# Scores of the output factor through SBUF, and the exponentials of a batch in one place of each engine's order

## The chip, the core and the metric

The kernel runs on one core of a Trainium2 chip as one program. The metric is the device time of an execution in microseconds (us). Five engines work from queues of their own: TensorE (PE), VectorE (DVE), ScalarE (ACT), GpSimd (POOL) and SyncE (SP), which here issues the transfers. The kernel writes the order of the instructions on each engine itself; at run time an instruction starts when its engine is free and the semaphores that it waits for have come.

## The reference

```python
# q, k, v: (4, 8, 576, 64)
q_lm, k_lm = means of 18 neighbouring rows            # 32 landmarks
A  = sm(q, k_lm); Bm = sm(q_lm, k_lm); C = sm(q_lm, k) # sm: max subtracted, exp, divided by sum
Z  = Bm.T / (norm1(Bm) * norminf(Bm) + 1e-6)
for _ in range(6): Z = 2 * Z - Z @ Bm @ Z
x  = A @ Z @ C @ v                                     # then rows of (2304, 512)
h  = x @ w_in;  x = (h * cos(h)) @ w_out               # d_ff 2048
h  = x @ w_in2; return (max(h, 0) + alpha * min(h, 0)) @ w_out2
```

## The kernel before

**Stages.** Four batches go through attention and through the first pair of layers. Each batch has two units of four heads (`unit(u, ...)`, units 0 and 1 for batch 0, 2 and 3 for batch 1, and so on) and one landmark matrix with its iterations (`z_path(b, ...)`). A unit transposes k and q (L594), forms the scores of the factor C (L670, "scores of the output factor": landmark queries against all keys), takes their maximum and exponential (L685 to L694), transposes the exponentials (L700, L704) and multiplies them by v (L715). It then forms the scores of A and their softmax (L742 to L757). `z_path` makes B, and iterates on it and on the product of C and v together: L851 is one Newton-Schulz step, and the first of these steps needs both units' products of L715. The weight that leaves `z_path` gives the operands of L909, and these feed the layers.

**Ticks.** The first pair of layers is cut into 128 ticks, each with six L949 matmuls into a PSUM tile `h`, an ACT and DVE chain for h cos(h) (L954 k, L956, L958 Sin, L959 square, L960, L963), and twelve L976 matmuls into `acc`. The tile `h` has two buffers: L949 of a tick waits for L960 of two ticks earlier. The units and the `z_path` of batches 1 to 3 are worked on between ticks: batch 1 from the start, batches 2 and 3 from ticks 36 and 66. The second pair of layers (L1235, L1316) follows.

**The planner.** Nothing of this order is written by hand. `Plan.op` takes operations with the buffers they read and write, `after` adds orders that no buffer forces, and `Plan.go` (L114) repeatedly picks, of the operations that are ready, the one that its table of durations lets start first, with a small term for its due time. An operation that needs another ACT function set than the current one is lengthened by 1.28 and its due time moved (L217). So a change of durations, of buffers or of `after` moves instructions on every engine.

**ACT function sets.** Exp belongs to one set and Sin to another. When consecutive ACT operations need different sets, an ACT_TABLE_LOAD stands between them.

**The tile `raw`.** It has three places, taken in turn by all its users: the loads of weights that are to be converted (`convert`, L465: 512 KB each, then three DVE operations L471, L473, L475), and, for batches 1 to 3, the k, q and v of each unit (L552, L568, L569). A place is taken again when the last reader of its user is done: L475 for a weight, L594 for k and q, L715 for v. All these loads go through the one queue that SP issues from, in order.

Of the kernel before, what the change touches and what calls it, by code (L numbers as in the profile page):

```python
# [258 lines left out]
def kernel(  # L259
# [267 lines left out]
    def unit(u, tu):  # L527
# [159 lines left out]
        op(dve(2), lambda e: nc.vector.tensor_reduce(nm_.t, mx.t, axis=AX.X, op=ALU.max, negate=True),  # L687
           r=[mx], w=[nm_])
        ce = atb(m, "ce", [P, R0, 2, 64])
        for ch in range(2):  # L690
            n = (N0, N1)[ch]
            op(("ACT", n / 1200.0 + 0.18), lambda e, ch=ch, n=n: nc.scalar.activation(
                ce.t[:, 0:n // 64, ch, :], sc[ch].t[:, 0:n].rearrange("p (r s) -> p r s", s=64),
                AF.Exp, bias=nm_.t, accum_out=sm.t[:, ch:ch + 1]), r=[sc[ch], nm_], w=[ce, sm], aset="exp")  # L694
# [66 lines left out]
    def z_path(b, tz):  # L761
# [620 lines left out]
```

## Time and profile before

| | |
|---|---|
| time, median of 3 runs | 882.39 us (881.43 to 885.32) |
| the profiled execution | 881.18 us |
| its span, first to last instruction | 879.4 us |
| busy: PE / DVE / ACT / POOL | 825.8 / 646.4 / 483.9 / 198.2 us |
| mean granted TensorE clock | 0.984 |

The busy time of PE says how long some matmul was in flight, not how fast it went. Where PE is idle or its clock is below 1.00, another engine or a transfer was late. The stretches that matter here are from 72 us (where the changed order first differs) to some 376 us (where the attention of batch 3 is over).

### The profile page before, as it was taken

The numbers are of one execution on the slowest core, as the hardware profiler recorded it, in microseconds if no ns is written. First come the engines' busy times: TensorE is split into PE (matmuls) and PEld (weight loads), VectorE is DVE, ScalarE is ACT, GpSimd is POOL, SyncE is SP. The second block draws the span as 40 slices with busy tenths as digits, with TensorE's granted clock in tenths as the row PEclk, the third lists the DMA queues.
The fourth block names the chain that finished last, engine by engine and source line by source line (L and its number), as shares of the span: only waits on it lengthen the run. The fifth ranks groups of instructions, "written<-read, shape, count | busy, mean of one in ns | idle before, by whom it ended". The sixth has DMA issues, their size and how long they took to land.

```text
span 879.4 us, 15395 instructions
## 1 busy us (share of the span) xinstructions
PE 825.8 (94%) x5681; PEld 726.3 (83%) x5681; DVE 646.4 (74%) x1279; ACT 483.9 (55%) x1118; POOL 198.2 (23%) x220
## 2 busy tenths in 40 slices
PE   5677899999999998999989999999999999999997
PEld 4436789888798887897889888889999999999996
DVE  4989969987896889768998777775665566555563
ACT  4467757777875687667678534443344334333431
POOL 1224511333321332114432222200120012000110
PEclk8989999999999999999999999999999999999999
DMA  8476506775359846666555111140113011310231
GB/s 233 116 215 143 171 26 189 229 178 136 123 159 268 230 119 196 186 182 218 182 185 181 51 48 48 61 132 25 37 61 85 25 37 60 85 37 25 66 115 24
DMA packets 89051, 107.44 MB, mean 122 GB/s; under 512 B 35984, under 2 KB 63120, under 8 KB 88976
## 3 DMA queue, kind: packets, MB, share of 16 engines
q1 hardware_dynamic: 88976, 106.46, 41.2%
q8 instruction: 44, 0.72, 0.3%
q14 instruction: 31, 0.25, 0.1%
HBM read 82.06 MB, written 24.38 MB: 121 GB/s over the span
## 4 chain that ended last, share of the span: by engine, by line
PE 61%; DVE 19%; DMA 10%; issue 3%; ACT 3%; SPq 1%; POOL 1%; DVEq 0%; POOLq 0%; ACTq 0%
PE acc L1316 21%; PE acc L976 10%; PE h L1235 9%; PE x L1235 7%; PE h L949 5%; DMA m<-in_moe_w_in_dram 4%; DMA m<-in_moe_w_out_dram 3%; DVE m L323 3%; DVE m L475 3%; DVE m L473 3%; PE x L909 2%; DMA m<-wi2d 2%; DVE m L471 2%; DVE m L960 2%; DVE m L956 2%
## 5 line engine op out<-in xcount | busy, mean ns | idle before, releaser
L976 PE MATMUL acc<-m,m 128*128 128x288 f32 x1536 | 238.0, 301 | 7.0 <-DVE m L323 3.4
L323 POOL TENSOR_TENSOR m<-m,m 128x288 fp32r<-128x288 f32 (+3 forms) x129 | 126.0, 984 | 459.7 <-ACT m L963 233.5
L976 PEld LDWEIGHTS acc<-m,m 128*128 128x128 f32 x1536 | 213.7, 190 | 18.4 <-issue 7.7
L1316 PE MATMUL acc<-m,m 128*128 128x512 f32 x864 | 207.5, 392 | 0.7 <-DVE m L323 0.4
L323 DVE TENSOR_TENSOR m<-m,m 128x512 fp32r<-128x512 f32 (+4 forms) x271 | 170.3, 651 | 34.9 <-ACT m L1184 9.3
L1316 PEld LDWEIGHTS acc<-m,m 128*128 128x128 f32 x864 | 158.9, 189 | 31.9 <-DVE m L323 0.9
L949 PE MATMUL h<-m,m 128*128 128x288 f32 x768 | 131.8, 307 | 14.9 <-DVE m L960 12.8
L949 PEld LDWEIGHTS h<-m,m 128*128 128x128 f32 x768 | 109.6, 191 | 34.9 <-DVE m L960 19.9
L1304 ACT ACTIVATE m<-m 128x512 fp32r<-128x512 f32 (+1 forms) x80 | 46.3, 588 | 111.5 <-DVE m L1302 109.0
L1235 PE MATMUL h<-m,m 128*128 128x256 f32 x768 | 106.9, 282 | 0.7 <-ACT m L318 0.6
L1235 PEld LDWEIGHTS h<-m,m 128*128 128x128 f32 x768 | 99.7, 189 | 3.6 <-ACT m L318 1.3
L1258 DVE TENSOR_TENSOR m<-h,m 128x512 f32<-128x512 f32 x32 | 22.1, 690 | 81.8 <-ACT m L318 78.9
L1235 PE MATMUL x<-m,m 128*128 128x256 f32 x576 | 80.3, 283 | 1.7 <-ACT m L318 1.7
L963 ACT ACTIVATE m<-m 128x288 fp32r<-128x288 f32 x128 | 55.8, 441 | 40.5 <-DVE m L960 35.4
L1235 PEld LDWEIGHTS x<-m,m 128*128 128x128 f32 x576 | 73.1, 188 | 3.4 <-ACT m L318 1.9
L318 ACT ACTIVATE m<-h 128x256 f32<-128x256 f32 (+2 forms) x93 | 36.8, 396 | 67.2 <-PE h L1235 58.9
L958 ACT ACTIVATE m<-m 128x288 f32<-128x288 f32 x128 | 55.6, 440 | 26.4 <-DVE m L956 26.0
L960 DVE SCALAR_TENSOR_TENSOR m<-m,h 128x288 f32<-128x288 f32 x128 | 56.5, 446 | 15.1 <-ACT m L959 14.8
L1095 ACT ACTIVATE m<-m 128x512 fp32r<-128x512 f32 x68 | 41.4, 628 | 45.0 <-PE h L1235 19.4
L954 ACT ACTIVATE m<-h 128x288 int32<-128x288 f32 x128 | 51.4, 404 | 22.8 <-PE h L949 22.0
L956 DVE SCALAR_TENSOR_TENSOR m<-h,m 128x288 f32<-128x288 f32 x128 | 57.0, 448 | 3.4 <-ACT m L954 3.2
L959 ACT ACTIVATE m<-m 128x288 f32<-128x288 f32 x128 | 55.2, 439 | 2.4
(150 smaller groups left out, 897.5 us busy)
## 6 DMA issues: line engine op xcount, KB each, us to landing
m<-in_moe_w_in_dram SPq DMA_DIRECT2D x32, 512.0 KB, 5.4
m<-in_moe_w_out_dram SPq DMA_DIRECT2D x32, 512.0 KB, 4.4
m<-wi2d SPq DMA_DIRECT2D x56, 256.0 KB, 3.5
m<-w1d SPq DMA_DIRECT2D x32, 256.0 KB, 5.5
y1d<-m SPq DMA_DIRECT2D x24, 288.0 KB, 2.8
out_dram<-m SPq DMA_DIRECT2D x36, 128.0 KB, 2.4
w1d<-m SPq DMA_DIRECT2D x16, 256.0 KB, 5.3
wi2d<-m SPq DMA_DIRECT2D x16, 256.0 KB, 2.9
```

Of the source, the lines that this page charges most:

```text
L323: ENG[e].tensor_tensor(o, a, b, op=ALU.subtract)
L949: nc.tensor.matmul(out=hp.t[:, 0:CW], lhsT=w_[:, js], rhs=x[:, cs], start=(i == 0), stop=(i == 5))
L954: op(act(CW, True), lambda e: nc.scalar.activation(k_.t, hp.t[:, 0:CW], AF.Copy, scale=INV2PI), r=[hp], w=[k_], target=T + 0.8)
L956: op(dve(CW), lambda e: nc.vector.scalar_tensor_tensor(u.t, hp.t[:, 0:CW], INV2PI, k_.t, op0=ALU.mult, op1=ALU.subtract), r=[hp, k_], w=[u])
L958: op(act(CW), lambda e: nc.scalar.activation(u.t, u.t, AF.Sin, scale=math.pi), rw=[u], aset="sin")
L959: op(act(CW), lambda e: nc.scalar.activation(u.t, u.t, AF.Square, scale=math.sqrt(2.0)), rw=[u])
L960: op(dve(CW), lambda e: nc.vector.scalar_tensor_tensor(hc.t, u.t, 1.0, hp.t[:, 0:CW], op0=ALU.subtract, op1=ALU.mult, reverse0=True), r=[h ...
L963: op(act(CW), lambda e: nc.scalar.activation(gh.t, hc.t, AF.Copy), r=[hc], w=[gh, gl])
L976: nc.tensor.matmul(out=yg[o].t[:, 0:CW], lhsT=w_.t[:, sl], rhs=x.t, start=(j == ja and i == 0), stop=(j == jb and i == 2),)
L1235: nc.tensor.matmul(out=rv(k), lhsT=a_.t[:, p, c2, js], rhs=b_.t[:, q_, c2, 0:hw], start=(first and c2 == 0 and i == 0), stop=(c2 == 1 and ...
L1304: op(act(w), lambda e, m_=m_, gh=gh: nc.scalar.activation(gh.t[:, 0:w], m_.t[:, 0:w], AF.Copy), r=[m_], w=[gh, gl])
L1316: nc.tensor.matmul(out=ya[n][t].t, lhsT=gv(x_), rhs=r_.t, start=(st and k == 0), stop=(en and k == 2))
```

## The change

In the units of batches 1 to 3 (`m` is 1 there) the scores of C no longer stay in PSUM until their exponential is done. Each half is copied to the SBUF tile `ce` by ACT or DVE, one reduction over all 576 columns gives the negated maximum (before: two maxima in PSUM and one over the pair), and one exponential in place, with its sum accumulated, takes the place of two. Room for a second `ce` comes from `wt`, which goes from four to two buffers.

New `after` orders per batch: the first exponential of C waits for the maximum of the second unit and for the subtraction in `z_path`; the second exponential of C follows the first; the first exponential of A waits for the subtraction of the second unit; the second unit's transposes follow the first's; the loads of v come behind the loads of k and q of both units. An ACT operation that needs another function set while it is not yet due gets 1.0 added to its key in the planner (`SP`). Units 0 and 1 keep their computation.

```diff
+KN: SP=1.0
                     key = s + KA * min(dl - s, KC)
+                    if o.aset and o.aset != cur and o.dl > s:
+                        key += KN["SP"]
...
-    at = at_raw = lay(0, at, ("wt", 4, 1024))
+    at = at_raw = lay(0, at, ("wt", 2, 1024), ("cex", 1, CE))
...
-        loads(4, ldv, 1.64, w=[vn], after=aft)
+        marks["vl", b, c] = loads(4, ldv, 1.64, w=[vn], after=aft)
...
+            if m:
+                ce = ce or atb(m, "ce", [P, R0, 2, 64])
+                op(pe(n, 4), cs, r=[kt, kqb[p][1]], w=[sc[ch]])
+                op([act(n, True), dve(n)], lambda e, ch=ch, n=n: copy(
+                    e, ce.t[:, 0:n // 64, ch, :], sc[ch].t[:, 0:n].rearrange("p (r s) -> p r s", s=64)),
+                   r=[sc[ch]], w=[ce])
+                continue
...
+            marks["cn", b, c] = op(dve(S), lambda e: nc.vector.tensor_reduce(
+                nm_.t, ces(), axis=AX.X, op=ALU.max, negate=True), r=[ce], w=[nm_])
+            marks["ce", b, c] = op(("ACT", S / 1200.0 + 0.18), lambda e: nc.scalar.activation(
+                ces(), ces(), AF.Exp, bias=nm_.t, accum_out=sm.t[:, 0:1]), r=[nm_], rw=[ce], w=[sm], aset="exp")
...
+        marks["vl", b, 0].after += gates["ld"]
+        marks["ce", b, 0].after += [marks["cn", b, 1], marks["zs", b]]
+        marks["ce", b, 1].after += [marks["ce", b, 0]]
+        marks["et", b, 1].after += [marks["et", b, 0]]
+        marks["vl", b, 1].after += [marks["vl", b, 0]]
+        marks["ae", b, 0].after += [marks["as", b, 1]]
```

The order of every engine moves from there. Three places are shown. In rows of the change the line numbers are those of the changed file: L469 is L465 of before, L572 and L573 are L568 and L569, L556 is L552, L705 the new exponential of C, L774 is L749 (A), L825 is L800 (B), L721 and L725 are L700 and L704, L736 is L715, L1001 is L976, L862 is L837, L320 is L318.

ACT, batch 1, before: the exponentials of B, of A and of C of unit 3 (those of unit 2 stand 39 rows earlier, behind a load of their own).

```order
L800 ACT_TABLE_LOAD
L800 ACTIVATE m_69<-m_69 128x64
L318 ACTIVATE m_1006<-acc 128x288
L959 ACTIVATE m_479<-m_479 128x288
L954 ACTIVATE m_479<-h 128x288
L318 ACTIVATE m_1006<-acc 128x288
L318 ACTIVATE m_1026<-acc 128x288
L749 ACTIVATE m_69<-m_69 128x576
L692 ACTIVATE m_175,m_69<-x,m_69 128x5x64
```

ACT, batch 1, in the change:

```order
L774 ACT_TABLE_LOAD
L774 ACTIVATE m_69<-m_69 128x576
L705 ACTIVATE m_175,m_69<-m_175,m_69 128x576
L825 ACTIVATE m_69<-m_69 128x64
L705 ACTIVATE m_433,m_69<-m_433,m_69 128x576
L320 ACTIVATE m_157<-x 128x512
L320 ACTIVATE m_157<-x 64x128
```

All exponentials of the batch stand behind one load, and those of C wait for the second unit. In the whole order of ACT there are 24 loads of tables before and 8 in the change, one pair for each of batches 1 to 3.

SP, batch 1, before (what an instruction waits for stands in brackets; m_157 is `raw`):

```order
L465 DMA m_157<-in_moe_w_out_dram 128x1024 [waits DMAHW5_49,DMAHW6_49,DMAHW4_49,PE_49]
L552 DMA m_157<-in_q_dram 64x9x64 [waits DMAHW7_49,DVE_49]
L552 DMA m_157<-in_q_dram 64x9x64 x2
L552 DMA m_157<-in_q_dram 64x9x64 [waits DMAHW0_49]
L465 DMA m_157<-in_moe_w_out_dram 128x1024 [waits DMAHW2_49,DMAHW3_49,DMAHW1_49,PE_49]
L465 DMA m_157<-in_moe_w_out_dram 128x1024 [waits DMAHW4_49,DVE_49]
L1212 DMA alpha_sb<-in_moe_alpha_dram 128x16x1
L465 DMA m_157<-in_moe_w_out_dram 128x1024 [waits DMAHW6_49,DMAHW5_49,DMAHW7_49,DMAHW0_49,PE_49]
L568 DMA m_157<-in_v_dram 64x2x320 [waits DMAHW1_49,DVE_49]
```

SP, batch 1, in the change, the stretch up to the v of unit 3:

```order
L572 DMA m_157<-in_v_dram 64x2x320 [waits DMAHW5_49,PE_49]
L573 DMA m_157<-in_v_dram 64x2x256 [waits DMAHW7_49,DMAHW6_49]
L572 DMA m_157<-in_v_dram 64x2x320 [waits PE_49]
L573 DMA m_157<-in_v_dram 64x2x256 [waits DMAHW0_49]
L469 DMA m_157<-in_moe_w_out_dram 128x1024 [waits DMAHW1_49,DVE_49]
L1243 DMA alpha_sb<-in_moe_alpha_dram 128x16x1 [waits DMAHW2_49]
L469 DMA m_157<-in_moe_w_out_dram 128x1024 [waits DMAHW4_49,DMAHW3_49,PE_49]
L469 DMA m_157<-in_moe_w_out_dram 128x1024 [waits DMAHW6_49,DMAHW5_49,DMAHW7_49,DMAHW0_49,PE_49]
L572 DMA m_157<-in_v_dram 64x2x320 [waits DMAHW1_49,DVE_49]
```

The v of unit 2 moved from ahead of the k of unit 3 to behind its q. Counted through the three places of `raw`, the weight just ahead of the v of unit 3 takes the place of the v of unit 2, so it is issued after unit 2's product L736, and the v of unit 3 stands behind it in the queue.

PE, batch 3, before, around unit 7's product with v (unit 6's stands 99 rows earlier; numbers tell buffers apart, m80896 is `raw`):

```order
L704 MATMUL x_3785<-m203008_69,m186624_175 64x128
L976 MATMUL acc_3199<-m111872_504,m151808_1795 128x288 x3
L976 MATMUL acc_3180<-m111872_504,m151808_1795 128x288 x3
L670 MATMUL x_3800<-m186624_175,m203008_69 64x320 x2
L670 MATMUL x_3801<-m186624_175,m203008_69 64x256 x2
L976 MATMUL acc_3187<-m111872_504,m151808_1795 128x288 x3
L976 MATMUL acc_3193<-m111872_504,m151808_1795 128x288 x3
L715 MATMUL x_3819<-m80896_157 32x64 x20
L976 MATMUL acc_3199<-m111872_504,m151808_1795 128x288 x3
```

PE, batch 3, in the change, from unit 6's product to unit 7's (m81408 is `raw`):

```order
L736 MATMUL x_3772<-m81408_157 32x64 x20
L1001 MATMUL acc_3190<-m112384_505,m152320_1716 128x288 x3
L721 MATMUL x_3805<-m203520_69,m76800_433 128x128 x4
L1001 MATMUL acc_3196<-m112384_505,m152320_1716 128x288 x3
L725 MATMUL x_3818<-m203520_69,m76800_433 64x128
L736 MATMUL x_3838<-m81408_157 32x64 x20
L862 MATMUL x_3864<-m203520_69 128x128 x2
L974 MATMUL h_3874<-m41984_440,m25600_436 128x288
```

Unit 7's product came 99 rows behind unit 6's and now comes six L1001 and one set of transposes behind it. Counted through the three places of `raw`, the v of unit 7 now takes the place of the v of unit 6, and the first and third of its four transfers wait for PE; before it took the place of a weight.

## Rows read from the trace of the kernel before

**Rows 1.** Stretches: length, busy of PE, PEld, DVE, ACT, POOL, PE clock, DMA.
```profile
72.00:126.00 54.00, 46.59 (x386) 40.95 (x385) 45.01 (x105) 35.85 (x84) 20.91 (x21) 0.94 0.44 114
126.00:200.00 74.00, 71.94 (x500) 63.62 (x499) 65.30 (x128) 54.29 (x138) 20.36 (x19) 1.00 0.61 178
200.00:300.00 100.00, 97.28 (x757) 84.23 (x755) 80.95 (x192) 73.18 (x167) 26.28 (x34) 1.00 0.65 184
300.00:376.00 76.00, 71.23 (x571) 61.10 (x570) 64.11 (x147) 53.70 (x125) 22.81 (x31) 1.00 0.58 175
376.00:880.00 504.00, 489.88 (x3140) 443.63 (x3138) 334.51 (x586) 229.91 (x524) 89.76 (x89) 0.99 0.27 85
```
**Rows 2.** What PE waited for from 72 to 126 us: total, times, longest.
```profile
PE h L949 <- DVE m L960: 3.8, 2, 3.6
PE x L700 <- ACT m L692: 1.5, 1, 1.5
```
**Rows 3.** Groups by line and form, table loads: count, busy us, mean ns.
```profile
L958 ACT ACT_TABLE_LOAD x12 | 15.4, 1283 | 0.2
L692 ACT ACT_TABLE_LOAD x5 | 6.4, 1283 | 4.1 <-DVE m L687 4.1
L749 ACT ACT_TABLE_LOAD x4 | 5.1, 1283 | 0.1
L800 ACT ACT_TABLE_LOAD x2 | 2.6, 1283 | 0.0
```
**Rows 4.** ACT in order of time around one table load: start, us.
```profile
80.25 1.28 ACT L958 ACT_TABLE_LOAD   x1
81.55 0.78 ACT L958 ACTIVATE m<-m 128x288 f32<-128x288 f32 x2
```
**Rows 5.** Groups by line and form: exponentials and maxima of C and A.
```profile
L692 ACT ACTIVATE m<-x,m 128x320 f32<-128x320 f32 x6 | 3.2, 527 | 0.1
L749 ACT ACTIVATE m<-m 128x576 f32<-128x576 f32 x8 | 5.5, 683 | 4.8 <-POOL m L323 4.8
L685 DVE TENSOR_REDUCE m<-x 128x1 f32<-128x320 f32 x6 | 2.9, 486 | 0.9 <-PE x L670 0.8
L747 DVE TENSOR_REDUCE m<-m 128x18 f32<-128x576 f32 x8 | 5.9, 743 | 0.1
```
**Rows 6.** PE and SP in order of time, unit 2's product, the loads behind, unit 7's product.
```profile
80.29 1.55 PE L715 MATMUL x<-m 128*32 128x64 f32 x40
81.88 0.33 SPq L465 DMA_DIRECT2D m<-in_moe_w_out_dram  x1
...
94.21 0.33 SPq L465 DMA_DIRECT2D m<-in_moe_w_out_dram  x1
...
96.96 0.61 SPq L569 DMA_DIRECT2D m<-in_v_dram  x1
...
343.26 1.00 PE L715 MATMUL x<-m 128*32 128x64 f32 x40 [0.21 <-DVE m L742]
```
**Rows 7.** Time from issue to landing: loads of v, and of weights to convert.
```profile
DMA to landing us min/median/max: 2.6/4.5/8.0
...
m<-in_moe_w_out_dram SPq DMA_DIRECT2D x32, 512.0 KB, 4.4
```
**Rows 8.** Groups by line and form: first and last operation of a conversion.
```profile
L475 DVE SCALAR_TENSOR_TENSOR m<-m,m 128x512 int32<-128x512 int32 x64 | 52.2, 818 | 0.5
L471 DVE TENSOR_SCALAR m<-m 128x512 int32<-128x512 int32 x64 | 34.0, 536 | 19.5 <-DMA m<-in_moe_w_in_dram 12.4 <-DMA m<-in_moe_w_out_dram 5.0 <-DMA m<-w1d 1.3
```
**Rows 9.** PE in order of time, batch 1's first Newton-Schulz step.
```profile
113.58 0.89 PE L851 MATMUL x<-m 128*128 128x192 f32 x4
```
**Rows 10.** PE in order of time, a stall at 402 us and a clean tick.
```profile
402.87 1.50 PE L949 MATMUL h<-m,m 128*128 128x288 f32 x6 [1.37 <-DVE m L960]
404.21 2.82 PE L976 MATMUL acc<-m,m 128*128 128x288 f32 x12
...
414.95 1.76 PE L976 MATMUL acc<-m,m 128*128 128x288 f32 x12
```

More of the change, by code (lines that the diff above doesn't have):

```diff
@@ L18 @@
 INV2PI = 1.0 / (2.0 * math.pi)
-KN = dict(T0=46, TA=3.4, TBT=3.05, VE=4.0, U1=-1, U2=36, U3=66, UD=7, UZ=20, C2=48, CD=2.3, LA=4, SW=6.0, BL=0.9, PB=0.2, AB=0.2, LM=126, JG=8, VG=8, AG=8, KA=0.004, KC=25, DRY=0)
+KN = dict(T0=46, TA=3.4, TBT=3.05, VE=4.0, U1=-1, U2=36, U3=66, UD=7, UZ=20, C2=48, CD=2.3, LA=4, SW=6.0, BL=0.9, PB=0.2, AB=0.2, LM=126, JG=8, VG=8, AG=8, SP=1.0, KA=0.004, KC=25, DRY=0)
 ADJ = {}
@@ L340, in lay @@
         return at
+    CE = 4 * R0 * P
     at = lay(0, 0, ("f", 4, 4 * FW), ("wo", 8, 2048))
@@ L346 @@
     at = at_wh = lay(0, at, ("wi", 8, 2048))
-    at = at_raw = lay(0, at, ("wt", 4, 1024))
-    CE = 4 * R0 * P
+    at = at_raw = lay(0, at, ("wt", 2, 1024), ("cex", 1, CE))
     at = lay(0, at, ("raw", 3, 4 * RAW))
@@ L360 @@
     KT, ST = 4 * NR * P, [("cmx", 2, 16), ("cnm", 2, 16), ("csm", 2, 16), ("crs", 2, 16), ("amx", 2, 80), ("asm", 2, 80)]
-    at_z = lay(1, at_1, *att(1, ("kt", 1, KT), ("qt", 2, KT), ("ce", 1, CE), ("at", 2, 4 * S), ("lt", 1, 256), *ST))
+    ST1 = [("cnm", 2, 8), ("csm", 2, 8), ("crs", 2, 8), ("amx", 2, 72), ("asm", 2, 72)]
+    at_z = lay(1, at_1, *att(1, ("kt", 1, KT), ("qt", 2, KT), ("ce", 1, CE), ("at", 2, 4 * S), ("lt", 1, 256), *ST1))
     at_0 = lay(0, at_w + 2048, *att(
@@ L374 @@
     at_end = at
+    place["1ce"] = (1, CE, place["1ce"][2] + place.pop("cex")[2])
     for tag, n in (("h", 2), ("x", 2), ("acc", 4)):
@@ L521 @@
     py, Cc = {}, {}
-    wt, ah = {}, {}
+    wt, ah, marks = {}, {}, {}
     def atb(m, tag, shape):
@@ L674, in scores @@
             )
-        sc = pair()
-        mx, nm_, sm = atb(m, "cmx", [P, 2]), atb(m, "cnm", [P, 1]), atb(m, "csm", [P, 2])
+        sc = pair() if m == 0 else (psb("x"), psb("x"))
+        mx = None if m else atb(m, "cmx", [P, 2])
+        nm_, sm = atb(m, "cnm", [P, 1]), atb(m, "csm", [P, 2])
+        ce = None
         for ch in range(2):
@@ L686, in unit, with ces @@
                r=[sc[ch]], w=[mx])
[L687 to L694, printed above, removed]
+        if m:
+            def ces():
+                return ce.t.rearrange("p r t s -> p (r t s)")[:, 0:S]
+            marks["cn", b, c] = op(dve(S), lambda e: nc.vector.tensor_reduce(
+                nm_.t, ces(), axis=AX.X, op=ALU.max, negate=True), r=[ce], w=[nm_])
+            marks["ce", b, c] = op(("ACT", S / 1200.0 + 0.18), lambda e: nc.scalar.activation(
+                ces(), ces(), AF.Exp, bias=nm_.t, accum_out=sm.t[:, 0:1]), r=[nm_], rw=[ce], w=[sm], aset="exp")
+        else:
+            op(dve(2), lambda e: nc.vector.tensor_reduce(nm_.t, mx.t, axis=AX.X, op=ALU.max, negate=True),
+               r=[mx], w=[nm_])
+            ce = atb(m, "ce", [P, R0, 2, 64])
+            for ch in range(2):
+                n = (N0, N1)[ch]
+                op(("ACT", n / 1200.0 + 0.18), lambda e, ch=ch, n=n: nc.scalar.activation(
+                    ce.t[:, 0:n // 64, ch, :], sc[ch].t[:, 0:n].rearrange("p (r s) -> p r s", s=64),
+                    AF.Exp, bias=nm_.t, accum_out=sm.t[:, ch:ch + 1]), r=[sc[ch], nm_], w=[ce, sm], aset="exp")
         e1, e2 = bank(0), bank(1)
@@ L700, in et1 @@
                 nc.tensor.transpose(e1.t[:, r * P:(r + 1) * P], ce.t[:, r].rearrange("p t s -> p (t s)"), ident)
-        o1 = op(pe(512, 2), et1, r=[ce], w=[e1, et])
+        o1 = marks["et", b, c] = op(pe(512, 2), et1, r=[ce], w=[e1, et])
         op([act(512), dve(512)], lambda e: copy(e, et.t[:, 0:R1].rearrange("p r m -> p (r m)"), e1.t),
@@ L722, in unit @@
         rs = atb(m, "crs", [P, 2])
-        op(dve(2), lambda e: nc.vector.scalar_tensor_tensor(
-            rs.t[:, 0:1], sm.t[:, 0:1], 1e-9, sm.t[:, 1:2], op0=ALU.add, op1=ALU.add), r=[sm], w=[rs])
+        if m:
+            op(dve(2), lambda e: nc.vector.tensor_scalar_add(rs.t[:, 0:1], sm.t[:, 0:1], 1e-9), r=[sm], w=[rs])
+        else:
+            op(dve(2), lambda e: nc.vector.scalar_tensor_tensor(
+                rs.t[:, 0:1], sm.t[:, 0:1], 1e-9, sm.t[:, 1:2], op0=ALU.add, op1=ALU.add), r=[sm], w=[rs])
         op(dve(2), lambda e: nc.vector.reciprocal(rs.t[:, 1:2], rs.t[:, 0:1]), rw=[rs])
@@ L740, in unit @@
             o1 = op(pe(n, 4), asc, r=[qt, kqb[p][0]],
-               w=[sa[ch]] if ch else [*sa, at], after=[o1] if ch else [])
+               w=[sa[ch]] if ch else [sa[ch], at] if m else [*sa, at], after=[o1] if ch else [])
             op(dve(n), lambda e, ch=ch, n=n, sa=sa, at=at: nc.vector.transpose(
@@ L747, in unit @@
         op(dve(S), lambda e, mxa=mxa, at=at: nc.vector.reduce_max(mxa.t, at.t, axis=AX.X), r=[at], w=[mxa])
-        op(tt, lambda e, mxa=mxa, at=at: sub(e, at.t, at.t, mxa.t.to_broadcast([P, NBK, M])), r=[mxa], rw=[at])
-        op(act(S), lambda e, at=at: nc.scalar.activation(at.t, at.t, AF.Exp), rw=[at], aset="exp")
+        marks["as", b, c] = op(tt, lambda e, mxa=mxa, at=at: sub(
+            e, at.t, at.t, mxa.t.to_broadcast([P, NBK, M])), r=[mxa], rw=[at])
+        marks["ae", b, c] = op(act(S), lambda e, at=at: nc.scalar.activation(at.t, at.t, AF.Exp), rw=[at], aset="exp")
         op(dve(S), lambda e, sma=sma, at=at: nc.vector.reduce_sum(sma.t, at.t, axis=AX.X), r=[at], w=[sma])
@@ L797, in z_path @@
         vop(nm_, lambda e: nv.reduce_max(mx.t, pbv(), axis=AX.X), r=[pb], w=[mx])
-        vop(nm_, lambda e: nv.tensor_tensor(bm.t, pbv(), mx.t.to_broadcast([P, n, M]), op=ALU.subtract),
-            r=[pb, mx], w=[bm])
+        marks["zs", b] = op(dve(nm_), lambda e: nv.tensor_tensor(
+            bm.t, pbv(), mx.t.to_broadcast([P, n, M]), op=ALU.subtract), r=[pb, mx], w=[bm])
         op(act(nm_), lambda e: nc.scalar.activation(bm.t, bm.t, AF.Exp, scale=8.0), rw=[bm], aset="exp")
```

## The prediction

> **What bounds the kernel now.** I read the page, then its stretches, then what TensorE (PE) waits for in them. From 376 us on PE is in flight for 490 of 504 us [rows 1], and the orders of PE, DVE and ACT from tick 94 on (some 372 us) differ in little, so nothing large can come from there. Before 72 us the order is the same. What can be won lies between: PE is idle for 7.4 us from 72 to 126, 2.1 to 200, 2.7 to 300 and 4.8 to 376, together 17.0, and the clock of 0.94 in the first stretch is worth another 3.2 (54 x 0.06). In that first stretch, batch 1's attention, VectorE sets the pace: it is busy for 45.0 of 54 us, and half of PE's idle time ends with its L960 [rows 1, 2]. Behind 126 us PE is busy for 94 to 97% and what stalls it is paid for nearly in full.
>
> **The change, part by part.**
>
> *Table loads.* Before there are 12 + 5 + 4 + 2 and one at the start, 24; the order of the change has 8. That takes 16 x 1.283 = 20.5 us from ACT [rows 3]. ACT is not the bound (35.9 of 54, 54.3 of 74 us busy [rows 1]), so of this only what PE waits for is won: at most the idle time above, of which the row that names the exponential of C is 1.5 us [rows 2].
>
> A load costs its own length: the one at 80.25 is followed by the next function at 81.55, 1.30 us later [rows 4]. The Trainium skill (ScalarE: Activation LUTs, What ACT_TABLE_LOAD costs) adds a drain of 1.38 us to each switch, 2.66 in all; by it ACT would be relieved of 42.6 us, an estimate by that page. No drain shows between those two rows, so the measurement decides, and PE's idle time caps the gain either way.
>
> *Exponentials and maxima.* Six units lose two exponentials of some 0.5 (0.527 for the longer) and two reads of the sum, and get one. It lies between 0.527 and the 0.683 of the same 576 columns [rows 5], plus the read; I take 0.68. Twelve copies out of PSUM come in, 11 on ACT, at about the length of such an exponential without its read. ACT is about even on this, +-3 us, all under the 20.5 that it loses. VectorE gives up two maxima (0.486 for the longer) and a short one per unit, and gets one reduction over 576 columns from SBUF, between 0.486 and the 0.743 of L747 [rows 5]: about -1 us in all, +-2. In the place where it matters this is used up: up to the end of batch 1's iterations VectorE now has seven subtractions of a tick's low part where it had three.
>
> *The waits that are added.* The first exponential of C now waits for the second unit's maximum. Behind it in ACT's queue stand the second exponential, B's and A's, and the copies of the transposes; behind those the Sin of the next ticks, hence L960 and the next `h`. PE's queue has few ticks' matmuls there.
>
> *The loads of v.* Loads go through one queue in order, and `raw` has three places. A place held by a v comes free with L715: the weight's load at 81.88 follows the end of that product at 80.29 + 1.55 by 0.04 us [rows 6]. Before, 12 us and more lay between such a load and the product that needs what is behind it. In the change two places have lost that distance.
>
> Batch 1: the weight ahead of the v of unit 3 waits for unit 2's product. From such a weight to the last of the four v transfers is 96.96 - 94.21 = 2.75 us [rows 6], and a v lands 4.5 us after issue (2.6 to 8.0 [rows 7]). So unit 3's product starts 7.3 us after the end of unit 2's (5.4 to 10.8), and PE has only five transposes, B's product and one tick's L949 for that time.
>
> When does this begin? VectorE passes 72.5 us in both. From there to unit 3's maximum it has 51 instructions in the change, 15 of them of conversions between 0.536 and 0.818 [rows 8], the others at the stretch's mean of 45.0/105 = 0.43 [rows 1]: 15 x 0.72 + 36 x 0.43 = 26.3, so 98.8 us, and up to 3.3 more where a converted weight is late (its load takes 4.4 to land [rows 7] and is now issued behind the loads of unit 3). The first exponential ends 0.9 later, T = 99.7 to 103. The second exponential and the copies take 1.8, the product 0.9 to 1.0 [rows 6], then 7.3 for the v, 0.9 for unit 3's product and 1.8 for twelve L976 [rows 10] that stand ahead of the first Newton-Schulz step: T + 12.7 = 112.4 to 115.7, against 113.58 [rows 9]. But at that step PE has done 96 of the L976 instead of 120. Those 24 still have to be done, and PE is the bound from then on: 24 x 1.76/12 = 3.5 us [rows 10]. Together +2.3 to +5.6; I take +3.5, nearer to the lower end, as the late weights are the least certain.
>
> Batch 3: the v of unit 7 waits for unit 6's product. Its last transfer is issued 2.05 us later and lands at 6.6 (4.7 to 10.1). PE has six L976 and five transposes for that, 1.3 us; the wait is 5.3 (3.4 to 8.8). VectorE's division by the sums (L729) stands in its queue ahead of the L960 that the next tick needs, so some 0.9 more passes in two steps. 6.2 in place of the 4.8 that is idle there now (which I count as gone): +1.4, from -0.5 to +4.9.
>
> The traced landing of a v is 2.6 at the least and 4.5 in the middle [rows 7], and I go by the middle. The Trainium skill (DMA: Bandwidth & Descriptors, Anatomy of one DMA) gives about 2 us of fixed cost for a transfer that GpSimd issues, and the rest by its bytes; SP issues these. By that estimate a v would land in 2.4 us, the waits would be some 2 us shorter each, and the sum about 4 lower. The trace has no landing that short, so the measurement decides.
>
> *The clock.* After a stall of 1.37 us the six matmuls at 402.87 took 1.50 and the next twelve 2.82, where a clean tick has 1.76 [rows 10]: the lower level of 1.2 GHz for some time. The six cost 1.50 - 0.88 (half of a clean twelve) = 0.6 and the twelve 2.82 - 1.76 = 1.1, together 1.7. The two long waits come in front of work that PE is the bound of: 0 to 1.7 each. I take 0.9 in batch 1, where the mean clock is 0.94 already [rows 1], and 1.7 in batch 3.
>
> *Batch 2.* Its loads of v hang on transposes in the change, not on a product, and 36 L976 stand ahead of the first transposes, so ACT's block is covered. Of the 2.7 us idle there I count none as won, +-2.
>
> **Sum.** 3.5 + 0.9 + 1.4 + 1.7 = +7.5. The profiled execution took 881.18 us (span 879.4 and 1.8 around it), so 888.7, rounded to 889. It lies 1.2 below the median of 882.39, which is inside the runs' own spread. The lows (2.3, 0, -0.5, 0 and -2 for batch 2) give 881, the highs (5.6, 1.7, 4.9, 1.7, 2) 897. That is the forecast's own range.
>
> **Rivals.** 0.5% is about what can be told from no change: 878.0 and 886.8 are its bounds around the median.
>
> 1. *The table loads decide, faster.* The place is every tick's chain from k over Sin to L960, which no longer has a load in it during attention. If the landing of v is as at its minimum or PE's other work covers it, and half of the 17.0 + 3.2 us comes back, it is 881.2 - 10.1 = 871. It is the case from the point where the two waits for v together stay under 4 us. For it speaks that 3.8 us of waiting hang on L960 [rows 2] and that L976 now stand more evenly between ticks; against it that no load stands in the 74 us from 126 on, which has its stalls all the same, and the two product pairs.
>
> 2. *The waits are covered, no change.* In batch 3 ACT's block of six exponentials and their copies takes some 10 us, and the next `h` waits for a Sin behind it. The matmuls ahead of unit 7's product last 8 us. If the block ends later than the v lands, PE waits for it alone, 10 - 8 = 2 us in place of 6.2, and the clock stays up: 2 - 4.8 = -2.8 instead of +3.1. Batch 1 keeps its 3.5 without the clock: 881.2 + 0.7, so 882. Against it: v is issued only after unit 6's product, near the end of those 8 us.
>
> 3. *VectorE, slower still.* It is busy for 65.3 of 74 us behind 126 [rows 1]. Up to tick 32 the order of the change gives it only 3 instructions more (314 for 311), but 7 more of them are of conversions (89 for 82): 7 x 0.72 [rows 8] = 5 us. If VectorE becomes the bound of that stretch, this comes on top: 889 + 5 = 894.
>
> That the change doesn't do what it says is excluded by the order for the loads; but the exponentials come in one group per batch, not two.
>
> **Chances.** The forecast 0.52, rival 1 0.15, rival 2 0.23, rival 3 0.10. The range runs from 875 to 897: it takes in the forecast and rival 2, most of rival 3 and the slower edge of rival 1. Faster by over 0.5%: rival 1 and a little of rival 2, 0.17. Within: the rest of rival 2 and the lower third of the forecast's range, 0.28. Slower: 0.55.
>
> **What would show it.** In the profile after: 8 table loads. PE waiting at the product L736 for in_v, some 5 us in batch 3 and some 3 in batch 1, each right after the other unit's product; the issue of that v within 0.1 us of a product's end (batch 3) or behind a weight that is (batch 1). The first Newton-Schulz step of batch 1 between 112 and 116 us with eight ticks of L976 done. A clock under 1.00 behind the wait in batch 3. It is wrong if those products start without a wait, if the step comes before 110, or if PE's idle time from 300 to 376 us falls below 4.

## The result

The changed kernel took 892.06 us (median of 4 runs, 890.14 to 892.81) against 881.91 for the kernel before (4 runs, 879.7 to 885.32): a ratio of 1.0105 with a 95% interval of 1.0076 to 1.0134. It is slower, by about 9 us; 889 had been forecast, with a range of 875 to 897. The profiled execution took 891.61 us, its span is 889.8, 10.4 more than before.

In rows of the changed file L974 is L949 of before, L983 the Sin (L958), L985 is L960, L876 the Newton-Schulz step (L851), L753 the division by the sums (L732), L831 a transpose of `z_path`, and L703 the one maximum of C.

Two stretches of the changed kernel, with the columns and edges of [rows 1]:

```profile
72.00:126.00 54.00, 45.92 (x357) 39.67 (x357) 44.86 (x103) 34.31 (x85) 13.21 (x15) 0.86 0.45 124
...
300.00:376.00 76.00, 70.70 (x567) 61.08 (x566) 60.90 (x142) 52.14 (x128) 26.58 (x33) 0.98 0.55 160
```

From 72 to 126 us PE is busy about as long as before, but has issued 357 matmuls and not 386, at a clock of 0.86 and not 0.94. Equal edges mislead here, since the same work lies later in the slower kernel. So from here on stretches are matched: their edges are where PE has done as much matmul work (each shape of matmul counted at its usual time) as the kernel before at 60, 126, 200, 300 and 376 us. Before, batch 1, then the changed kernel:

```profile
60.00:126.00 66.00, 55.63 (x444) 48.11 (x443) 56.40 (x122) 43.46 (x104) 28.61 (x29) 0.95 0.51 142
```

```profile
61.99:132.35 70.36, 59.33 (x438) 49.98 (x438) 57.54 (x125) 43.49 (x105) 20.10 (x22) 0.88 0.46 133
132.35:206.64 74.29, 72.14 (x505) 65.04 (x505) 63.64 (x121) 53.98 (x137) 23.68 (x25) 1.00 0.62 180
206.64:308.63 101.99, 96.87 (x757) 84.10 (x756) 77.49 (x183) 67.09 (x165) 22.07 (x30) 1.00 0.62 179
308.63:384.71 76.08, 71.17 (x570) 61.86 (x570) 58.50 (x136) 50.88 (x126) 25.26 (x32) 0.98 0.55 168
```

That is +2.0 us up to the first edge, +4.4 in batch 1, +0.3, +2.0 in batch 2, +0.1 in batch 3, and the rest, +1.7, behind. All of these are differences of two single executions. The clock's share of a stretch, (1 - clock) times its length, is 3.3 us in batch 1 before and 8.4 after; PE's idle time there is 10.4 and 11.0.

What PE waits for, from 72 to 126 and then from 308.63 to 384.71 us (answers to [rows 2]):

```profile
PE h L974 <- DVE m L985: 3.3, 2, 2.9
PE x L862 <- ACT m L320: 1.6, 1, 1.6
PE x L725 <- DVE m L753: 0.8, 1, 0.8
PE x L736 <- DMA m<-in_v_dram: 0.7, 1, 0.7
PE x L736 <- ACT m L320: 0.6, 1, 0.6
...
PE x L736 <- DMA m<-in_v_dram: 3.1, 2, 2.1
PE h L974 <- DVE m L985: 1.7, 1, 1.7
```

The waits for v are there, 0.7 and 3.1 us where none was. The table loads, of [rows 3], and the exponentials and the maximum of C, of [rows 5]:

```profile
L983 ACT ACT_TABLE_LOAD x4 | 5.1, 1283 | 0.1
L705 ACT ACT_TABLE_LOAD x2 | 2.6, 1283 | 0.0
L433 ACT ACT_TABLE_LOAD x1 | 1.3, 1283 | 0.7 <-PEq L1395 0.7
L774 ACT ACT_TABLE_LOAD x1 | 1.3, 1283 | 0.0
...
L705 ACT ACTIVATE m<-m,m 128x576 f32<-128x576 f32 x6 | 4.6, 767 | 0.0
L703 DVE TENSOR_REDUCE m<-m 128x1 f32<-128x576 f32 x6 | 4.5, 752 | 0.8 <-ACT m L320 0.4
```

Eight loads, 20.5 us less on ACT, as counted; an exponential of C takes 0.767 and not the 0.68 that I took, its maximum 0.752.

PE in batch 1, in order of time (the waits stand in brackets), and the loads on SP beside it:

```profile
102.67 0.66 PE L721 MATMUL x<-m,m 128*128 128x128 f32 x4 [0.34 <-ACT m L705]
103.16 0.27 PE L725 MATMUL x<-m,m 128*64 128x128 f32 x1
104.06 1.00 PE L736 MATMUL x<-m 128*32 128x64 f32 x40 [0.62 <-ACT m L320]
104.98 0.66 PE L721 MATMUL x<-m,m 128*128 128x128 f32 x4
106.42 0.30 PE L725 MATMUL x<-m,m 128*64 128x128 f32 x1 [0.79 <-DVE m L753]
108.29 1.22 PE L862 MATMUL x<-m 128*128 128x128 f32 x4 [1.57 <-ACT m L320]
109.17 1.79 PE L974 MATMUL h<-m,m 128*128 128x288 f32 x6
110.88 0.43 PE L736 MATMUL x<-m 128*32 128x64 f32 x4
112.03 1.44 PE L736 MATMUL x<-m 128*32 128x64 f32 x36 [0.72 <-DMA m<-in_v_dram]
113.40 3.25 PE L1001 MATMUL acc<-m,m 128*128 128x288 f32 x12
116.45 1.31 PE L876 MATMUL x<-m 128*128 128x192 f32 x4
```

```profile
105.10 0.33 SPq L469 DMA_DIRECT2D m<-in_moe_w_out_dram  x1
105.52 0.61 SPq L572 DMA_DIRECT2D m<-in_v_dram  x1
...
107.47 0.61 SPq L573 DMA_DIRECT2D m<-in_v_dram  x1
```

The weight is issued 0.04 us after unit 2's product ends (104.06 + 1.00), the v behind it, and unit 3's product is in full 7.0 us after that end. Behind a row of waits of 0.3 to 1.6 us the twelve L1001 take 3.25 where a clean twelve takes 1.76 [rows 10]. The first Newton-Schulz step comes at 116.45. In batch 3 the same pair:

```profile
350.01 0.94 PE L736 MATMUL x<-m 128*32 128x64 f32 x40
...
354.56 0.31 PE L736 MATMUL x<-m 128*32 128x64 f32 x4 [2.07 <-DMA m<-in_v_dram]
355.93 1.07 PE L736 MATMUL x<-m 128*32 128x64 f32 x36 [1.07 <-DMA m<-in_v_dram]
```

```profile
350.98 0.60 SPq L572 DMA_DIRECT2D m<-in_v_dram  x1
...
352.97 0.60 SPq L573 DMA_DIRECT2D m<-in_v_dram  x1
```

### The profile page after: what moved, and what is told of

It is laid out like the page before. It is cut to its first block, busy times and chain, and to the rows that moved or that the text cites. A ratio compares the mean times of both kernels' runs of the same rounds, so it can differ in the third digit from the quotient of the medians.

```text
span 889.8 us, 15352 instructions
## 1 busy us (share of the span) xinstructions
PE 829.5 (93%) x5681; PEld 730.5 (82%) x5681; DVE 637.0 (72%) x1256; ACT 474.6 (53%) x1118; POOL 188.7 (21%) x215
## 4 chain that ended last, share of the span: by engine, by line
PE 64%; DVE 14%; DMA 11%; ACT 3%; issue 3%; SPq 3%; POOL 1%; DVEq 0%; POOLq 0%; ACTq 0%
PE acc L1347 20%; PE acc L1001 12%; PE h L1266 9%; PE x L1266 7%; PE h L974 6%; DMA m<-in_moe_w_in_dram 4%; DMA m<-in_moe_w_out_dram 3%; DVE m L325 2%; DVE m L477 2%; PE x L934 2%; DMA m<-wi2d 2%; DVE m L479 2%; DVE m L985 1%; PE x L598 1%; DVE m L475 1%
## 5 line engine op out<-in xcount | busy, mean ns | idle before, releaser
L1001 PE MATMUL acc<-m,m 128*128 128x288 f32 x1536 | 238.4, 302 | 5.5 <-DVE m L1021 2.0
L1001 PEld LDWEIGHTS acc<-m,m 128*128 128x128 f32 x1536 | 215.9, 191 | 16.5 <-issue 7.6
L325 POOL TENSOR_TENSOR m<-m,m 128x288 fp32r<-128x288 f32 (+3 forms) x127 | 121.1, 960 | 475.5 <-ACT m L988 202.8
L974 PE MATMUL h<-m,m 128*128 128x288 f32 x768 | 133.5, 309 | 16.1 <-DVE m L985 14.6
L974 PEld LDWEIGHTS h<-m,m 128*128 128x128 f32 x768 | 110.5, 192 | 35.7 <-DVE m L985 22.9
L1266 PEld LDWEIGHTS h<-m,m 128*128 128x128 f32 x768 | 99.4, 189 | 3.4 <-ACT m L320 1.1
L985 DVE SCALAR_TENSOR_TENSOR m<-m,h 128x288 f32<-128x288 f32 x128 | 57.3, 448 | 27.8 <-ACT m L984 27.0
L320 ACT ACTIVATE m<-h 128x256 f32<-128x256 f32 (+2 forms) x93 | 36.9, 396 | 67.0 <-PE h L1266 58.1
L983 ACT ACTIVATE m<-m 128x288 f32<-128x288 f32 x128 | 56.4, 442 | 27.1 <-DVE m L981 26.3
L984 ACT ACTIVATE m<-m 128x288 f32<-128x288 f32 x128 | 56.4, 442 | 3.0
```

What stands on the lines that cost most here:

```text
L325: ENG[e].tensor_tensor(o, a, b, op=ALU.subtract)
L974: nc.tensor.matmul(out=hp.t[:, 0:CW], lhsT=w_[:, js], rhs=x[:, cs], start=(i == 0), stop=(i == 5))
L983: op(act(CW), lambda e: nc.scalar.activation(u.t, u.t, AF.Sin, scale=math.pi), rw=[u], aset="sin")
L984: op(act(CW), lambda e: nc.scalar.activation(u.t, u.t, AF.Square, scale=math.sqrt(2.0)), rw=[u])
L985: op(dve(CW), lambda e: nc.vector.scalar_tensor_tensor(hc.t, u.t, 1.0, hp.t[:, 0:CW], op0=ALU.subtract, op1=ALU.mult, reverse0=True), r=[h ...
L1001: nc.tensor.matmul(out=yg[o].t[:, 0:CW], lhsT=w_.t[:, sl], rhs=x.t, start=(j == ja and i == 0), stop=(j == jb and i == 2),)
```

## The experiments

Ratios are against the kernel before on the same chip, with 95% intervals. "Own order" means that every engine's order is that of the kernel it came from, so that only the edit differs; "planned anew" means that the planner made another order. The columns of stretches are matched ones in us; "L976 done" counts those on PE ahead of batch 1's first Newton-Schulz step, and the column before it says when that step begins, from the first edge. Two things limit the comparison. The kernel before took 883.1 to 883.5 us on the chips of the experiments (median) and 881.9 beside the changed kernel, so the expected times, which were set against the latter, are some 1.2 to 1.6 us low there, and the ratio is the better measure. And every stretch is read from one execution: in the kernels of the same order a stretch differs by up to 1.8 us (changed, e1, e6, e8) or 0.7 (before, e2), and the profiled execution of n2, e5 and e6 lies 3.7, 3.4 and 1.6 us above the median, those of e7 and e9 2 below.

| kernel | ratio | batch 1 | 126-200 | batch 2 | batch 3 | step at | L976 done |
|---|---|---|---|---|---|---|---|
| before | 1 | 66.0 | 74.0 | 100.0 | 76.0 | 53.6 | 120 |
| changed | 1.0105 (1.0076 to 1.0134) | 70.4 | 74.3 | 102.0 | 76.1 | 54.5 | 96 |
| e1, changed, other v | 1.0089 (1.0069 to 1.0109) | 69.0 | 74.0 | 102.6 | 77.8 | 53.7 | 96 |
| e2, before, no loads | 0.9989 (0.9974 to 1.0005) | 65.7 | 74.6 | 99.4 | 76.7 | 53.5 | 120 |
| e3, not grouped | 1.0001 (0.9989 to 1.0013) | 65.2 | 75.6 | 103.0 | 72.4 | 49.9 | 114 |
| n2, before planned anew | 1.0054 (1.0036 to 1.0073) | 66.9 | 78.9 | 101.5 | 76.4 | 54.5 | 120 |
| e4, C free | 1.0014 (0.9996 to 1.0031) | 63.1 | 76.4 | 106.1 | 73.5 | 52.7 | 138 |
| e5, A free | 1.0048 (1.0030 to 1.0065) | 73.7 | 76.7 | 98.4 | 73.0 | 58.3 | 96 |
| e6, changed, no loads | 1.0078 (1.0047 to 1.0109) | 69.5 | 74.2 | 102.5 | 76.0 | 53.4 | 96 |
| e7, no new orders | 1.0050 (1.0031 to 1.0068) | 67.9 | 79.5 | 99.2 | 74.5 | 56.2 | 129 |
| e8, PE kept busy | 1.0078 (1.0055 to 1.0101) | 69.1 | 75.1 | 102.0 | 77.5 | 53.0 | 96 |
| e9, C gathered in batch 1 | 1.0049 (1.0031 to 1.0067) | 69.4 | 74.3 | 101.7 | 73.5 | 53.4 | 96 |
| e10, C gathered in 2 and 3 | 1.0061 (1.0043 to 1.0080) | 64.2 | 76.9 | 103.4 | 77.7 | 53.8 | 138 |
| e11, mixed | 1.0005 (0.9984 to 1.0026) | 64.1 | 77.7 | 101.7 | 74.8 | 53.7 | 138 |

**e1: is it the waits for v?** Own order of the changed kernel.

```diff
-                            rhs=vv_(vn)[0:n, bb, hh, r, :],
+                            rhs=et.t[0:n, r, 0:D] if m and c else vv_(vn)[0:n, bb, hh, r, :],
```

> The changed kernel in its own order, but the product of exponentials and v of the second unit of batches 1 to 3 multiplies by another tile in SBUF and not by v (its transfers are still issued; this part of the output is another number). So PE no longer waits for the transfers of v there. Theory A, the waits for v are the loss: the product of unit 7 loses its 3.1 us of waiting and that of unit 3 its 0.7, with a share of the clock the time falls by 3 to 5 us, to 887 to 889. Rival B, the block of exponentials and copies on ACT holds the next h in any case: PE waits for L985 instead, and the time falls by less than 1.5 us, to 890.5 to 892.

The time was 890.8 us, the ratio 0.16% under that of the changed kernel, with intervals that overlap. PE's waits in the matched stretch of batch 3:

```profile
PE h L974 <- DVE m L985: 2.4, 2, 2.1
PE x L862 <- DVE m L322: 2.1, 1, 2.1
PE x L736 <- ACT m L320: 0.6, 1, 0.6
```

The 3.1 us are gone and 5.1 of others stand in their place (4.8 with v). Theory A falls by these rows and by batch 3's stretch, which is 1.7 longer and not shorter; the time agrees with B, though intervals this wide would not tell 3 us from 1.5 by themselves. B's cause is not shown by it. Batch 1 is at 69.0, about what it is in e6 and e8, which have this order and still wait for v (69.5 and 69.1).

**e2: what are the loads worth?** Own order of the kernel before, `AF.Exp` replaced by `AF.Identity` in batches 1 to 3.

> The kernel before in its own order, with the exponentials of batches 1 to 3 replaced by a copy with the same operands (the softmax is left out there), so that 22 of its 24 table loads are gone and nothing else. Theory A, ACT is off the path: at most the 1.5 us of PE's waits that name the exponential and about 1 us elsewhere, so 879 to 882. Rival 1 of the prediction, the loads decide: half of the idle time of PE comes back, 871 to 875.

882.3 us beside 883.1: 0.11% less, and no change is inside the interval. Batch 2's stretch, columns as before:

```profile
200.88:300.30 99.42, 97.08 (x756) 84.17 (x755) 80.43 (x191) 60.47 (x157) 26.57 (x34) 1.00 0.66 185
```

ACT is busy for 60.47 us where it was for 73.18 [rows 1], and the stretch is 0.6 shorter. 22 loads taken away win at most 0.26%, so the 16 that the change removes had next to nothing to give. Rival 1 of the prediction is out.

**e3: without the gathering.** Planned anew.

```diff
-        marks["ce", b, 0].after += [marks["cn", b, 1], marks["zs", b]]
-        marks["ce", b, 1].after += [marks["ce", b, 0]]
-        marks["et", b, 1].after += [marks["et", b, 0]]
...
-        marks["ae", b, 0].after += [marks["as", b, 1]]
```

> The changed kernel without the four orders that gather the exponentials (first and second exponential of C, first of A, second unit's transposes); planned anew, 20 table loads. Theory G, the loss comes from gathering (both units' products fall together and L976 are left over at the first Newton-Schulz step): the time goes back to 882 to 885. Rival R, any new order of this plan costs about that much: it stays at 887 to 893.

882.8 us beside 883.1: the loss is gone, as theory G says, though scores still go through SBUF. It is a new order as well, and the next run shows what that alone can do.

**n2: what does a new order cost by itself?** The kernel before with `AB=0.22` in place of 0.2.

> The kernel before with one constant of the planner changed from 0.20 to 0.22 (by how much ACT is preferred over DVE); the computation is the same, the order moves. Theory G: a new order by itself costs little, 880 to 885. Rival R, the order of before is a lucky one: 886 to 892.

888.4 us, 0.54% slower with no change in what is computed. The profiled execution was the slowest of its six (892.08); of the 9.6 us by which its span is longer than before, 4.9 lie between 126 and 200 us:

```profile
127.46:206.37 78.91, 73.74 (x499) 63.76 (x498) 65.19 (x124) 54.72 (x139) 24.35 (x24) 1.00 0.59 169
```

So rival R has a part: half a per cent can come from a reshuffle, which is half of the loss to be explained, and a run that is planned anew says little by its time and more by its stretches. One such reshuffle was measured; how far others scatter isn't known.

**e4 and e5: C's order or A's?** Planned anew, each without the first or the last line of e3's edit alone. Both have 14 table loads.

> The changed kernel without one order alone: the first exponential of C no longer waits for the maximum of the second unit and the subtraction of z_path. Planned anew: 14 table loads, exponentials of A still gathered. Unit 2's and unit 3's products stand 63 matmuls of L1001 apart instead of none, those of batch 3 84 instead of 6. Theory G1, this one order brings the products together and is the whole loss: 880 to 884. Rival G2, the gathering of A's exponentials and the loads of v have a good part in it: 885 to 889. Rival R, a new order costs by chance: 886 to 892.

> The changed kernel without the order that the first exponential of A waits for the second unit's subtraction; C's are still gathered. Planned anew: 14 table loads, as in the run beside it, but the products of a batch's two units still stand next to each other. Theory G1: no gain, 889 to 893. Rival G2, A's part matters: 884 to 888. Were the number of table loads what counts, this run and the one beside it would come out alike.

885.3 and 887.6 us. Freeing C brings 0.9 of the 1.05%, freeing A 0.6. As measured both times lie in G2's ranges; by the ratio e4 would be 883.1 where the ranges were set (1.0014 x 881.9), in G1's, and e5 886.1, in G2's still. So by the times neither theory is clean. Batch 1's stretches of the two:

```profile
60.59:123.69 63.10, 52.93 (x443) 45.07 (x442) 54.18 (x117) 43.08 (x101) 24.44 (x27) 1.00 0.54 149
```

```profile
60.61:134.27 73.66, 59.39 (x438) 49.39 (x438) 55.39 (x124) 45.02 (x106) 20.78 (x24) 0.88 0.45 127
```

With C free the stretch is the shortest of all, with A free the longest. The execution of e5 that was profiled took 890.97 us, hardly less than the changed kernel's; its batches 2 and 3 are shorter (98.4 and 73.0), but where the gain of the median comes from isn't shown. The number of table loads, the same in both, is not what tells them apart.

**e6: is ACT's block what holds PE?** The edit of e2 in the changed kernel, own order.

> The changed kernel in its own order, with the exponentials of batches 1 to 3 replaced by a copy with the same operands (softmax left out there): 2 table loads in place of 8. ACT's block of a batch, which holds the next Sin, is then 2.6 us shorter, one load ahead and one behind. Theory B, that block is what PE waits for: 2 us in each of batches 1 and 3, so 887 to 889. Rival, PE waits for the chain of transposes, copies and products whatever ACT's block takes: 890.5 to 892.

890.7 us, in the rival's range as measured, in B's by the ratio (1.0078 x 881.9 = 888.8). Batches 1 to 3 are at 69.5, 102.5 and 76.0, within a microsecond of the changed kernel. So a block that is 2.6 us shorter shows in no stretch, where B wanted 2 us in each of batches 1 and 3, and theory B is not borne out; the ratio alone, 0.27% (2.4 us) under the changed kernel's with overlapping intervals, would not exclude it. One more thing shows in this trace, in batch 1:

```profile
108.33 1.79 PE L974 MATMUL h<-m,m 128*128 128x288 f32 x6
...
112.06 1.87 PE L1001 MATMUL acc<-m,m 128*128 128x288 f32 x12
```

PE's waits ahead of these rows are nearly those of the changed kernel (0.8, 0.8, 1.6 and, for v, 0.5 us), but the clock is back for the twelve (3.25 there), and the stretch is no shorter than e1's, where they took 2.98.

**e7: the rest of the change.** Planned anew without the six new orders; 16 loads.

> The changed kernel with none of the new orders (neither the exponentials' nor the loads' of v): scores of C through SBUF, two places for wt and the planner's 1.0 for an early change of function set. Planned anew: 16 table loads, products of a batch 81, 57 and 105 L1001 apart. Theory G1: no loss, 880 to 884, and 8 loads fewer than before bring nothing either. Rival, the copies through SBUF and the loss of two places of wt cost by themselves: 886 to 890.

888.1 us, 0.5% slower, in the rival's range and not in G1's. In the profiled execution 126 to 200 has +5.5, the stretch in which n2 has +4.9, and batch 1 +1.9. Whether the copies cost something or the order does can't be told by this run; e3, which has the copies too, is even with before.

**e8: is it the clock?** Own order of the changed kernel, with 36 matmuls more on PE; one of the four places:

```diff
+            if b == 1:
+                for _ in range(3):
+                    nc.tensor.matmul(out=pc.t[:, 0:P], lhsT=ident, rhs=ident, start=True, stop=True, skip_group_check=True)
             for r in range(R0):
```

> The changed kernel in its own order, with extra matmuls of the identity by itself put into PE's queue in batch 1 where PE waits: 1 ahead of each unit's transposes, 3 ahead of each product with v, 4 ahead of unit 3's last transpose, 6 ahead of the product in z_path, into banks that the next instruction overwrites. Theory K, the loss of batch 1 is the clock that falls in the row of short waits: the clock's share of that stretch (8.5 us in the changed kernel, 3.3 before) falls under 5 and the time by 2 to 4 us against the changed kernel, to 887 to 889. Rival W, the waits themselves are the loss: the extra matmuls cost their own time, 892 to 894.

```profile
107.20 1.05 PE L987 MATMUL h<-m,m 128*128 128x288 f32 x6
...
110.89 1.87 PE L1014 MATMUL acc<-m,m 128*128 128x288 f32 x12
```

```profile
59.59:128.64 69.05, 60.09 (x474) 51.05 (x474) 57.65 (x125) 43.60 (x105) 20.10 (x22) 0.95 0.48 136
```

The rows are PE's in order of time (L987 is L974, L1014 is L1001) and batch 1's stretch. The clock is kept: 1.05 us for the six in place of 1.79, 1.87 for the twelve in place of 3.25, and its share of the stretch falls from 8.4 to 3.5, as K says. The time, 890.0, is in neither range as measured; by the ratio it is 888.8, in K's, and 2.4 us under the changed kernel. But e6, in which nothing was done for the clock, has the same ratio (1.0078). The stretch is 69.1, as long as e1's:

```profile
60.89:129.94 69.05, 58.38 (x438) 49.09 (x438) 56.94 (x125) 43.38 (x105) 20.16 (x22) 0.90 0.47 136
```

Idle 9.0, clock 3.5 and the 4.8 us of the extra matmuls (start to next start) are 17.3 in which PE does nothing useful; in e1 idle and clock are 10.7 and 6.9, together 17.6. So the balance is what it would be if the low clock only filled time that PE would have waited anyway. That reading isn't shown: an extra matmul that stood in the way would have cost what the clock gave back, and one execution of each can't tell a gain of some 1 us.

**e9 and e10: which batch?** Planned anew, the first line of e3's edit behind `if b == 1:` or `if b > 1:`.

> The changed kernel with C's first exponential waiting for the second unit in batch 1 alone; planned anew, 12 table loads. Theory G1, the loss is batch 1's: its stretch (before 66.0, changed 70.4 us for the same matmuls) stays at 69 to 74, batch 3's is 72 to 75, the time 885 to 890. Rival V, the loss is in batches 2 and 3, where the products stand closest: batch 1's stretch is under 68 and the time 880 to 884.

> The changed kernel with C's first exponential waiting for the second unit in batches 2 and 3 alone; planned anew, 10 table loads. Theory G1: batch 1's stretch is 63 to 66 and the time 880 to 885. Rival V: batch 3's stretch is 76 or more (it waits for the v of unit 7), batch 2's 102 or more, and the time 886 to 890.

Batch 3's stretch in e9, then in e10, with PE's waits in the latter:

```profile
306.19:379.65 73.46, 70.65 (x571) 60.89 (x571) 58.11 (x131) 52.44 (x129) 26.45 (x33) 1.00 0.60 172
```

```profile
304.58:382.31 77.73, 72.70 (x571) 63.77 (x571) 58.46 (x136) 50.97 (x126) 24.95 (x32) 0.96 0.55 164
```

```profile
PE x L736 <- DMA m<-in_v_dram: 3.2, 2, 2.0
PE h L974 <- DVE m L985: 1.8, 1, 1.8
```

e9 (887.3 us) is as G1 says in all three numbers. e10 (888.8) has G1's stretch in batch 1 (64.2) but V's in batches 2 and 3 and V's time. So both are right for their place: with C gathered in batch 1 its stretch is 69.4 against 64.2, with C gathered in batch 3 that one is 77.7 against 73.5 (though e5, which gathers it too, has 73.0); batch 2 (103.4 against 101.7) is within what new orders scatter. Only batch 1's part stands over the whole table: every kernel with C gathered there has 69.0 to 73.7, every other 63.1 to 67.9. As times, the 0.49 and 0.61% of these two runs are about what the reshuffle n2 lost (0.54%). And the stretches behind one another are not independent. From the first edge to that of 200 us the kernel before takes 140.0 us, the changed one 144.7; e3, e4, e10 and e11 take 139.5 to 141.8, but n2 and e7, which gather nothing, 145.8 and 147.4.

**e11: a better version?** Planned anew: e3's first line out, the other three behind `if b == 1:`.

> A version made of the best stretches so far: C's exponentials free in all batches, A's exponentials, the second exponential of C and the second unit's transposes in order in batch 1 only, nothing of it in batches 2 and 3; 18 table loads. If the stretches add up (batch 1 63, batch 3 72 to 73), 877 to 881, faster than both kernels. Rival R, what a new order costs elsewhere takes it back: 882 to 888.

884.6 us beside 883.1, no difference, as rival R says. The stretches of batches 1 and 3 are under before (64.1 and 74.8, together by 3.1 us), batch 3's less than hoped; 126 to 200 is 3.7 longer, which takes it all back. No version here beats the kernel before.

## Why the prediction came out

The time lies in the range and on the forecast side, 3 us over the forecast. That the sum came so near is in part luck: batch 3's 3.1 did not come, and 5.7 came from three places that stood in the sum at nothing. Of the signs named, the eight loads, the 96 L976, the wait at L736 in both batches (shorter than said), the issue within 0.1 us and the clock under 1.00 in batch 3 came; the step came at 116.45, just behind the 112 to 116, and PE's idle time from 300 to 376 is 5.3, over the 4 that would have refuted it. By steps, with the span's +10.4 as what is to be explained:

- **Table loads: right.** 8 are left, 20.5 us of loads went from ACT, and e2 shows what the removed loads are worth: 0.26% at the most. To count them as won only where PE waits for ACT was the right reading of [rows 1, 2].
- **Batch 1, +3.5 and 0.9 for the clock: +4.4 measured (3.0 to 3.5 in e1, e6 and e8, the same order).** The debt is what was right. The step begins within a microsecond of where it began before (54.5 for 53.6; 53.0 to 53.7 in the three other profiles of this order), with 96 L976 done and not 120, and 24 x 0.147 = 3.5. Over the table the stretch follows that count: 69.0 to 73.7 with 96, 65.2 to 67.9 with 114 to 129, 63.1 to 64.2 with 138. That is in good part bookkeeping, as the stretch ends where an equal amount of work is done; it says where the time went and not yet why the step comes no earlier when so much less was done ahead of it.
- **The reason given for it was wrong in part.** The v of unit 3 came 7.0 us after unit 2's product (7.3 forecast), and T was 102.5 (99.7 to 103). But PE had waits of its own in those 7 us, 0.8 for VectorE's L753 and 1.6 for copies that a product of `z_path` (L862) needs, and only 0.7 was left for v. The step that failed is that the chain to the first Newton-Schulz step runs through v: without that wait (e1) the step comes at 53.7, no earlier than in e6 and e8 (53.4 and 53.0), which have it. What does set that chain isn't shown; taking away v's wait (e1), the loads on ACT (e6) or the low clock (e8) moved the step by 0.8 to 1.5 us against the changed kernel, which one execution of each can't tell from chance. The trace has a lead. Both waits go back to VectorE: the 0.8 names it, and the first of the copies behind the 1.6 had itself waited for it:

```profile
106.55 0.26 ACT L320 ACTIVATE m<-m 32x64 f32<-32x64 f32 x1 [0.62 <-DVE m L831]
```

VectorE is busy for 7.88 of the 8 us from 101 to 109. Whether a lighter VectorE there would bring the step forward was not tried.
- **The clock: mis-sized.** I added 0.9 and 1.7; its share grew by 5.1 and 1.5. With 5.1 beside the debt of 3.5 batch 1 would be 8.6 longer and not 4.4, so the two overlap; by how much isn't shown (e8).
- **Batch 3, +3.1: +0.1 measured (0 to +1.8 in the same order).** The v is issued 0.03 us behind unit 6's product as forecast, and PE waits for it, 3.1 and not 5.3: its last transfer is issued at 352.97 and the product goes on at 355.93, a landing of 3 us where I took 4.5. The measured +0.1 lies halfway between this +3.1 and rival 2's -2.8, and rival 2 had a point in the mechanism: without v, other waits take its place (e1). Against the orders with C free (72.4 to 74.8 in e3, e4, e7, e9, e11) the changed order is 1 to 5 us longer in batch 3, but e5, with C gathered, has 73.0; the kernel before has 76.0 there for other waits.
- **Batch 2, the stretch behind 376 us and the start: 0, 0 and 0 forecast, +2.0, +1.7 and +2.0 measured.** The start is the same order in all these kernels and the others have 59.6 to 60.9 there, so that is likely chance of one execution. Batch 2 had 2.0 to 2.6 in all four profiles of the changed order, but 101.5 to 106.1 in most orders planned anew, gathered or not. That a planner's new order costs by itself was no term of my sum and no rival; n2 puts it at some 5 us (0.36 to 0.73%). Three more kernels of the changed order (e1, e6, e8) have ratios of 1.0078 to 1.0089, so a part of the 1.05% may be chance of its four runs too.

What stays open: why 126 to 200 loses in most new orders and batch 2 too, what sets the chain of batch 1, and how much of the loss the gathering has beyond what any new order costs. That gathering C in batch 1 lengthens that stretch is shown; that it is the cause of the whole loss is not.

## What to carry to other kernels

Price what an engine saves at what others wait for in that stage, not at its own time: 28 us of table loads on ACT were worth 0.26% of the time at the most. An order that makes two independent units meet takes the filling work from between them: count, at the point where they meet, how much of the bound engine's other work is done by then, before and after. Where a greedy planner lays out the program, change a constant that means nothing first; here that moved the time by half a per cent, and it took stretches matched by work to tell a part of the edit's effect from the reshuffle's.

## What the hardware did that I had not expected

- Four waits of 0.3 to 1.6 us between 102.3 and 108.3 us, with matmuls between them, were followed by the lower of PE's two clocks, 1.2 GHz (granted 0.50 from 108 to 116 us; six L974 in 1.79 us, twelve L1001 in 3.25). How long it lasted varied: in e6, with nearly the same waits, the six took 1.79 and the twelve 1.87. With 36 extra matmuls in those places it was granted 1.00 throughout (106 to 114 us of e8; 1.05 and 1.87), and the stretch was 69.1 us, as in e1 without them.
- The v transfers from SP landed about 3 us after their issue in batch 3 (352.97 to 355.93) and 4.6 in batch 1 (107.47 to 112.03), taken to where the product that waited goes on. What made the second longer was not tried.
